# A fused attention and two-MLP kernel: the conversion of fp64 weight words moved off GpSimd, the second MLP's weights converted during the first and staged in device memory

## The chip, the core and the metric

The kernel runs on one core of one Trainium2 chip. The metric is the device time of the whole program in microseconds (us); a run takes some 1844 us.

## What is computed

Attention in chunks of 64 positions over q, k, v (batch 8, 8 heads, 576 positions, head size 64), then two MLPs on the 4608 resulting rows of 512 features. All weights arrive as fp64 words.

```python
attn = softmax(scale * q_c @ k_c^T)            # chunks of 64
x    = (attn @ v_c)                            # -> [4608, 512]
# first MLP, d_ff 1536
xn   = x / sqrt(mean(x*x) + 1e-6) * rms_g
g, v = xn @ w_gate, xn @ w_val
x    = (g * sigmoid(g) * v) @ w_out
# second MLP, d_ff 2048
h    = x @ w_in
P    = a0 + a1*h + a2*h^2 + a3*h^3
Q    = 1 + |b0|*|h| + |b1|*h^2
out  = (P / (Q + 1e-6)) @ w_out2
```

## The kernel before

The 4608 rows are worked in 9 blocks (`j`) of 512 rows. The first MLP runs over all blocks, then the second over all blocks; between them the rows wait in device memory (`x2d`). TensorE multiplies fp32 numbers as pairs: each operand is split into a rounded part (hi, type fp32r) and the remainder (lo), and each product is three matmuls of 128x512 (`PASSES`), so a product over 512 features is a group of 12 matmuls.

**First MLP.** In block `j`, for `f` in 0 to 11: `p1_gate` makes `g` (12 matmuls), ScalarE takes its tanh into `u` and VectorE multiplies (line 315); `p1_val` makes `vl` (12), VectorE multiplies (321), ScalarE casts hi of `r` (323) and VectorE subtracts for lo (324); `p1_gemm2` adds the product of an earlier `f` into the output accumulators `a` (12). `g` and `vl` share two PSUM buffers, so the next `g` needs the one that line 315 has read. Attention for the next block's four tiles of 128 rows is threaded between these groups by a plan of slots (three slots per `f`): matmuls `xs`, transposes `tp`, and work on VectorE, ScalarE and GpSimd. The first four tiles are done before the first block (`begin`, tiles named `start`).

**Second MLP.** Steps `s` over (`j`, `f`), `f` in 0 to 15: `h` (12 matmuls), a chain on ScalarE and VectorE, lo of `gg` on GpSimd (459), and three steps later `o` (12 matmuls).

**Weights.** `unit(u, w, keys)` brings three 128x512 weight tiles (1.5 MB of fp64 words) and converts them in place. Seen as 32-bit words, the high word is scaled by ScalarE as if it were fp32 (line 111) and the low word rounded to three bits (112). VectorE shifts the high word by three (114) and puts its sign back (115), GpSimd adds the two as integers (119), ScalarE casts hi (123), and lo is the difference (125), on VectorE for even units and on GpSimd for odd ones. 12 units serve the first MLP, 11 the second. The raw words and the converted pairs share 13 buffers of one size (`s3`), and the 12 units of the first MLP stay in them until its last block. So the units of the second MLP are converted in block 8, as the buffers of the first come free, and the tables `work` say at which slot each step of a unit is recorded.

In the first MLP a scheduler orders the instructions of each engine within these slots; in the second the order of ScalarE and VectorE is the written one. All DMAs are issued by SP, in one queue that waits in order.

Of the kernel before, what the change touches and what calls it, by code (L numbers as in the profile page):

```python
# [28 lines left out]
def fused_kernel(  # L29
# [66 lines left out]

    wt = {}

    def unit(u, w, keys):
# [6 lines left out]
        yield
        low, high = raw[:, :, :, 0], raw[:, :, :, 1]  # L110
# [462 lines left out]
```

## Time and profile before

| what | value |
|---|---|
| time, median of 3 runs | 1844.55 us (1843.34 to 1845.27) |
| the profiled execution: time, span | 1844.64 us, 1842.7 us |
| matmuls (PE) busy | 1779.6 us, 97% of the span |
| VectorE (DVE), ScalarE (ACT), GpSimd (POOL) busy | 1164.3, 901.5, 381.7 us |
| mean granted TensorE clock | 0.983 of full speed |

Time and span differ by 1.9 us, which lie around the profiled instructions. Busy time counts instructions that overlap at their ends as one; a matmul is in flight longer than the next one waits, so a busy PE is not a PE that could do no more. Where PE is gapless, the distance from one group of 12 matmuls to the next is the measure: 2.72 us.

### The profile page before, as it was taken

What the parts mean: (1) busy time and instruction counts of PE and PEld (TensorE: products, weight loads), DVE (VectorE), ACT (ScalarE), POOL (GpSimd) and SP (SyncE); (2) the same over time, 40 slices, a digit from 0 to 9 for tenths busy, and PEclk for the clock granted to TensorE, in tenths of its full rate; (3) what the DMA queues carried; (4) which work ended last, traced back from release to release, by engine and by line L of the source; (5) the groups of instructions that cost most, each with busy time, mean ns of one, the idle gap of its engine ahead of it and who ended that gap; (6) DMA issues with size and microseconds to landing.
All of it is one profiled execution on the core that took longest, in us unless ns stands there. A gap on an engine that the chain in (4) does not pass through costs nothing.

```text
span 1842.7 us, 24647 instructions
## 1 busy us (share of the span) xinstructions
PE 1779.6 (97%) x9948; PEld 1461.7 (79%) x9948; DVE 1164.3 (63%) x1602; ACT 901.5 (49%) x1408; POOL 381.7 (21%) x295
## 2 busy tenths in 40 slices
PE   4779999999999999999998899999999999999999
PEld 3668888888888888888887678888888888888887
DVE  6994444343344434434346698888787888888886
ACT  5653222222222222222235677767777776767675
POOL 3660000000000000000024442323232332233222
PEclk8889999999999999999999999999999999999999
DMA  7512111110011111101034400100101010101000
GB/s 297 200 52 69 58 34 42 35 58 24 30 58 35 42 34 58 30 23 58 1 115 140 149 20 5 42 29 18 35 12 35 12 40 7 40 7 46 1 23 23
DMA packets 41105, 93.86 MB, mean 51 GB/s; under 512 B 4640, under 2 KB 4640, under 8 KB 40992
## 3 DMA queue, kind: packets, MB, share of 16 engines
q1 hardware_dynamic: 40992, 92.30, 15.0%
q8 instruction: 78, 1.28, 0.3%
q14 instruction: 35, 0.29, 0.1%
HBM read 73.41 MB, written 18.87 MB: 50 GB/s over the span
## 4 chain that ended last, share of the span: by engine, by line
PE 87%; DVE 3%; issue 3%; POOL 2%; ACT 2%; POOLq 0%; DVEq 0%; ACTq 0%
PE o L469 21%; PE h L300 21%; PE g L300 14%; PE vl L300 14%; PE a L339 14%; PE xs L183 2%; POOL raw_i L119 1%; PE tp L228 1%; PE tp L225 1%; DVE raw_g L115 1%; POOL raw_q L119 0%; ACT w_i L123 0%; DVE r L324 0%; DVE t_g L114 0%; DVE raw_q L115 0%
## 5 line engine op out<-in xcount | busy, mean ns | idle before, releaser
L300 PE MATMUL g<-xT,w_g 128*128 128x512 f32 (+1 forms) x1308 | 320.1, 394 | 13.4 <-DVE u L315 11.3
L300 PE MATMUL vl<-xT,w_g 128*128 128x512 f32 x1296 | 322.1, 397 | 0.6 <-DVE u L321 0.6
L339 PE MATMUL a<-r,w_g 128*128 128x512 f32 x1296 | 316.5, 393 | 3.9 <-DVE r L324 2.7
L300 PEld LDWEIGHTS g<-xT,w_g 128*128 128x128 f32 x1308 | 248.2, 192 | 67.4 <-DVE u L315 13.6
L459 POOL TENSOR_TENSOR gg<-T,gg 128x512 fp32r<-128x512 f32 x144 | 187.5, 1302 | 509.7 <-ACT gg L458 417.4
L339 PEld LDWEIGHTS a<-r,w_g 128*128 128x128 f32 x1296 | 245.9, 190 | 56.4 <-DVE r L324 3.4
L300 PE MATMUL h<-x,w_i 128*128 128x512 f32 x1188 | 287.3, 391 | 2.9 <-DVE u L315 2.9
L315 DVE SCALAR_TENSOR_TENSOR u<-u,g 128x512 f32<-128x512 f32 x108 | 74.2, 687 | 341.5 <-ACT u L314 337.4
L300 PEld LDWEIGHTS vl<-xT,w_g 128*128 128x128 f32 x1296 | 241.1, 190 | 51.9 <-DVE u L321 1.8
L469 PE MATMUL o<-w_q,gg 128*128 128x512 f32 x1080 | 261.5, 391 | 2.3 <-ACT gg L458 1.4
L300 PEld LDWEIGHTS h<-x,w_i 128*128 128x128 f32 x1188 | 224.1, 189 | 50.0 <-DVE u L315 3.3
L469 PEld LDWEIGHTS o<-w_q,gg 128*128 128x128 f32 x1080 | 203.7, 189 | 45.5 <-ACT gg L458 1.9
L314 ACT ACTIVATE u<-g 128x512 f32<-128x512 f32 x108 | 64.6, 598 | 351.2 <-PE g L300 350.8
L438 ACT ACTIVATE V<-h 128x512 f32<-128x512 f32 x144 | 85.9, 596 | 181.7 <-PE h L300 181.5
L214 POOL TENSOR_SCALAR ssq<-ssq 128x1 f32<-128x1 f32 x36 | 8.8, 245 | 743.7 <-ACT xf L213 733.6
L469 PE MATMUL o<-w_i,gg 128*128 128x512 f32 x648 | 157.1, 391 | 0.0
L441 DVE SCALAR_TENSOR_TENSOR V<-V,small,R 128x512 f32<-128x512 f32 x144 | 108.3, 752 | 73.4 <-ACT R L439 73.4
L323 ACT CAST r<-u 128x512 fp32r<-128x512 f32 x108 | 67.1, 621 | 172.7 <-DVE u L321 172.6
L469 PEld LDWEIGHTS o<-w_i,gg 128*128 128x128 f32 x648 | 120.9, 188 | 27.7 <-DVE ob L480 2.3
L300 PE MATMUL h<-x,w_q 128*128 128x512 f32 x540 | 129.7, 389 | 0.0
L452 DVE SCALAR_TENSOR_TENSOR V<-V,R 128x512 f32<-128x512 f32 x144 | 125.6, 872 | 4.9
L451 DVE SCALAR_TENSOR_TENSOR V<-V,R 128x512 f32<-128x512 f32 x144 | 99.9, 693 | 44.9 <-ACT R L450 44.9
(118 smaller groups left out, 2032.3 us busy)
## 6 DMA issues: line engine op xcount, KB each, us to landing
raw_g<-in_w_dram SPq DMA_DIRECT2D x12, 1536.0 KB, 12.1
x2d<-x SPq DMA_DIRECT2D x36, 256.0 KB, 2.6
x2r<-x2d SPq DMA_DIRECT2D x36, 256.0 KB, 3.2
out_dram<-ob SPq DMA_DIRECT2D x36, 256.0 KB, 2.1
q<-in_qkv_dram SPq DMA_DIRECT2D x32, 256.0 KB, 2.7
k<-in_qkv_dram SPq DMA_DIRECT2D x32, 256.0 KB, 2.7
v<-in_qkv_dram SPq DMA_DIRECT2D x32, 256.0 KB, 2.9
raw_i<-in_w_dram SPq DMA_DIRECT2D x5, 1536.0 KB, 6.3
```

The costliest lines, as they stand in the source:

```text
L183: nc.tensor.matmul(out=ps[cc, hp, n, p, :], lhsT=lhsT, rhs=rhs, start=True, stop=True)
L300: nc.tensor.matmul(out=acc[:, ts], lhsT=w[:, wh, wk], rhs=x[:, kk, xh, ts], start=kk == 0 and n == 0, stop=kk == KD - 1 and n == 2,)
L314: nc.scalar.activation(out=u, in_=g, func=AF.Tanh, scale=0.5)
L315: nc.vector.scalar_tensor_tensor(out=u, in0=u, scalar=1.0, in1=g, op0=ALU.add, op1=ALU.mult)
L323: nc.scalar.copy(r[:, 0, :], u)
L339: nc.tensor.matmul(out=acc1[j][m], lhsT=wt["o", f][:, wh, ms], rhs=r[:, xh, :], start=f == 0 and n == 0, stop=f == NF1 - 1 and n == 2,)
L438: nc.scalar.activation(out=V, in_=h, func=AF.Square)
L441: nc.vector.scalar_tensor_tensor(out=V, in0=V, scalar=absb1, in1=R, op0=ALU.mult, op1=ALU.add)
L451: nc.vector.scalar_tensor_tensor(out=V, in0=V, scalar=1.0 + 1e-6, in1=R, op0=ALU.add, op1=ALU.mult)
L452: nc.vector.scalar_tensor_tensor(out=V, in0=V, scalar=-2.0, in1=R, op0=ALU.add, op1=ALU.mult)
L459: nc.gpsimd.tensor_tensor(out=r[:, 1, :], in0=T, in1=r[:, 0, :].bitcast(F32), op=ALU.subtract)
L469: nc.tensor.matmul(out=acc2[j][m], lhsT=r[:, rh, ms], rhs=wt["q", f][:, wh, :], start=f == 0 and n == 0, stop=f == NF2 - 1 and n == 2,)
```

## The change

The conversion becomes one helper, `words_to_pair`, on ScalarE and VectorE alone. ScalarE's first operation is Prelu with a slope for negative numbers: it scales a negative high word by another power of two than a positive one, so that the shift by three leaves the sign bit where it belongs. With that the operation that put the sign back is gone. The integer add of high and low is an instruction of VectorE (named ISA in the order, its operands as 1536 times 2 halves of a word), and lo is VectorE's for every unit. Unit 0 is brought and converted in three parts.

The second MLP's weights no longer wait for block 8. Each of the 32 tiles is a generator `stage(t)`: 512 KB come into the 13th buffer, the only one left beside the 12 units, are converted there, and the pair (512 KB) is written to device memory (`w2d`). In block 8 `unit2` loads three finished pairs by one DMA as each buffer comes free.

```diff
-    def unit(u, w, keys):
+    def words_to_pair(high, low, t, hi, lo):
+        nc.scalar.activation(
+            out=high.bitcast(F32), in_=high.bitcast(F32), func=AF.Prelu, scale=2.0 ** -112, alpha=2.0 ** 32
+        )
+        nc.scalar.mul(t.bitcast(I32), low, 2.0 ** -29)
+        yield
+        nc.vector.tensor_scalar(out=high, in0=high, scalar1=3, scalar2=None, op0=ALU.logical_shift_left)
+        nc.vector.tensor_tensor(out=high, in0=high, in1=t, op=ALU.add)
+        yield
+        x = high.bitcast(F32)
+        nc.scalar.copy(hi, x)
+        nc.vector.tensor_tensor(out=lo, in0=x, in1=hi.bitcast(F32), op=ALU.subtract)
+        yield
+
+    def unit(u, keys):
...
-        nc.scalar.mul(high.bitcast(F32), high.bitcast(F32), 2.0 ** -112)
-        nc.scalar.mul(low.bitcast(I32), low, 2.0 ** -29)
-        t = sb.tile([P, U, W], U32, tag="t", bufs=1, name=f"t_{name}")[:, :n]
-        nc.vector.tensor_scalar(out=t, in0=high, scalar1=3, scalar2=None, op0=ALU.logical_shift_left)
-        nc.vector.scalar_tensor_tensor(
-            out=high, in0=high, scalar=0x80000000, in1=t, op0=ALU.bitwise_and, op1=ALU.bitwise_or
-        )
-        yield
-        nc.gpsimd.tensor_tensor(out=high.bitcast(I32), in0=high.bitcast(I32), in1=low.bitcast(I32), op=ALU.add)
...
-        nc.scalar.copy(whole[:, :n, 0, :], x)
-        eng = (nc.vector, nc.gpsimd)[u % 2]
-        eng.tensor_tensor(out=whole[:, :n, 1, :], in0=x, in1=whole[:, :n, 0, :].bitcast(F32), op=ALU.subtract)
...
+        parts = [slice(t, t + 1) for t in range(n)] if u == 0 else [slice(0, n)]
...
+    w2d = [dram.tile([P, U, 2, W], F32, tag=f"w2d_{u}", name=f"w2d_{u}") for u in range(-(-2 * NF2 // U))]
+
+    def stage(t):
+        buf = s3(f"stage{t}")
+        raw = buf[:, 0].rearrange("p two f -> p (two f)").bitcast(U32)
+        pair = buf[:, 1]
+        nc.sync.dma_start(out=raw, in_=w2[t])
+        yield
+        raw = raw.rearrange("p (f two) -> p f two", two=2)
+        for _ in words_to_pair(raw[:, :, 1], raw[:, :, 0], buf[:, 2, 0].bitcast(U32), pair[:, 0, :], pair[:, 1, :]):
+            yield
+        nc.sync.dma_start(out=w2d[t // U][:, t % U], in_=pair.bitcast(F32))
+        yield
+
+    def unit2(u, keys):
+        whole = s3(f"w2_{u}")
+        n = len(keys)
+        nc.sync.dma_start(out=whole[:, :n].bitcast(F32), in_=w2d[u][:, :n])
...
+        span = (NB - 2) * 3 * NF1
+        for t in range(2 * NF2):
+            at = 3 * NF1 + t * span // (2 * NF2)
+            at_slots(stage(t), (at, at + 2, at + 3, at + 4, at + 5))
         for u, x in enumerate(second):
-            for at in (3 * u + 6 if u else 0, 3 * u + 8, 3 * u + 9, 3 * u + 10):
-                work.setdefault((NB - 1, at), []).append(x)
+            at_slots(x, ((NB - 1) * 3 * NF1 + 3 * u,))
```

The lines of the changed kernel have other numbers: the shift is 110, the add 111, lo 115; Prelu 105, the low word 108, the cast 114; tanh 347, the VectorE steps on `u` and `r` 348, 354 and 357, the cast of `r` 356.

**VectorE in the first block, `f` = 0 and 1** (before, then with the change; `raw_g_3` is unit 3's words, `w_g_2` unit 2's pair, `u0_1` block 0, `f` = 1). Before:

```order
L125 TENSOR_TENSOR w_g_2_499<-raw_g_2_106,w_g_2_499 128x3x512
L321 TENSOR_TENSOR u0_0_438<-u0_0_438,vl0_0_441 128x512
L114 TENSOR_SCALAR t_g_3_472<-raw_g_3_411 128x1536
L115 SCALAR_TENSOR_TENSOR raw_g_3_411<-raw_g_3_411,t_g_3_472 128x1536
L324 TENSOR_TENSOR r0_0_455<-u0_0_438,r0_0_455 128x512
L315 SCALAR_TENSOR_TENSOR u0_1_490<-u0_1_490,g0_1_477 128x512
L114 TENSOR_SCALAR t_g_4_536<-raw_g_4_475 128x1536
L321 TENSOR_TENSOR u0_1_490<-u0_1_490,vl0_1_502 128x512
L115 SCALAR_TENSOR_TENSOR raw_g_4_475<-raw_g_4_475,t_g_4_536 128x1536
L324 TENSOR_TENSOR r0_1_516<-u0_1_490,r0_1_516 128x512
```

With the change:

```order
L354 TENSOR_TENSOR u0_0_461<-u0_0_461,vl0_0_464 128x512
L270 RECIPROCAL den4_490<-den4_490 128x8
L111 ISA raw_g_3_433<-raw_g_3_433,t_g_3_494 128x1536x2
L357 TENSOR_TENSOR r0_0_478<-u0_0_461,r0_0_478 128x512
L115 TENSOR_TENSOR w_g_2_122<-raw_g_2_121,w_g_2_122 128x3x512
L348 SCALAR_TENSOR_TENSOR u0_1_513<-u0_1_513,g0_1_500 128x512
L110 TENSOR_SCALAR raw_g_4_497<-raw_g_4_497 128x1536
L354 TENSOR_TENSOR u0_1_513<-u0_1_513,vl0_1_524 128x512
L115 TENSOR_TENSOR w_g_3_434<-raw_g_3_433,w_g_3_434 128x3x512
L357 TENSOR_TENSOR r0_1_538<-u0_1_513,r0_1_538 128x512
L111 ISA raw_g_4_497<-raw_g_4_497,t_g_4_557 128x1536x2
```

The steps on `u` and `r` stand among the conversions as before, and the units are as far ahead. Per unit there were two VectorE instructions and, for every other unit, a third; now there are always three, and none on GpSimd between the second and the cast.

**ScalarE in block 1, `f` = 5 to 7** (`u1_5` is block 1, `f` = 5; `xf` and `p` are attention). Before:

```order
L314 ACTIVATE u1_5_1740<-g1_5_1727 128x512
L323 CAST r1_5_1763<-u1_5_1740 128x512
L314 ACTIVATE u1_6_1791<-g1_6_1778 128x512
L213 ACTIVATE xf10_1829,ssq10_1830<-xa10_1827 128x512
L200 ACTIVATE p11_1834<-p11_1834 128x512
L323 CAST r1_6_1853<-u1_6_1791 128x512
L314 ACTIVATE u1_7_1881<-g1_7_1868 128x512
```

With the change:

```order
L347 ACTIVATE u1_5_1773<-g1_5_1760 128x512
L105 ACTIVATE stage8_2904<-stage8_2904 128x512
L108 ACTIVATE stage8_2904<-stage8_2904 128x512
L356 CAST r1_5_1796<-u1_5_1773 128x512
L114 CAST stage8_2904<-stage8_2904 128x512
L347 ACTIVATE u1_6_1828<-g1_6_1815 128x512
L246 ACTIVATE xf10_1866,ssq10_1867<-xa10_1864 128x512
L105 ACTIVATE stage9_3083<-stage9_3083 128x512
L233 ACTIVATE p11_1871<-p11_1871 128x512
L108 ACTIVATE stage9_3083<-stage9_3083 128x512
L356 CAST r1_6_1892<-u1_6_1828 128x512
L114 CAST stage9_3083<-stage9_3083 128x512
```

Each `f` has the three ScalarE operations of one staged tile between its tanh and the next. The scheduler has put the 32 tiles earlier than their slots say: tile 0 behind the tanh of block 0, `f` = 7, tile 31 behind that of block 3, `f` = 8, so 31 tiles further on in 37 steps of `f`.

**SP in block 2** (`stage16` is tile 16's buffer, `w2d_5` the pairs of tiles 15 to 17). Before:

```order
L353 DMA x2d_1_69<-x2_1_0_2279 128x512
L353 DMA x2d_1_69<-x2_1_1_2282 128x512
L353 DMA x2d_1_69<-x2_1_2_2285 128x512
L353 DMA x2d_1_69<-x2_1_3_2288 128x512
L164 DMA q14_2373<-in_qkv_dram 128x512
L165 DMA k14_2374<-in_qkv_dram 128x512
L166 DMA v14_2375<-in_qkv_dram 128x512
```

With the change:

```order
L150 DMA stage16_4440<-in_w2_dram 128x1024
L155 DMA w2d_5_82<-stage16_4440 128x1024
L150 DMA stage17_4626<-in_w2_dram 128x1024
L155 DMA w2d_5_82<-stage17_4626 128x1024
L150 DMA stage18_4818<-in_w2_dram 128x1024
L197 DMA q15_2653<-in_qkv_dram 128x512
L198 DMA k15_2654<-in_qkv_dram 128x512
L199 DMA v15_2655<-in_qkv_dram 128x512
L155 DMA w2d_6_83<-stage18_4818 128x1024
```

Loading and writing alternate, one tile at a time, in the one queue, with the loads for attention between them.

**ScalarE in the last block, `f` = 7 to 9.** Before:

```order
L111 ACTIVATE raw_q_7_7553<-raw_q_7_7553 128x1536
L314 ACTIVATE u8_7_7568<-g8_7_7555 128x512
L112 ACTIVATE raw_q_7_7553<-raw_q_7_7553 128x1536
L323 CAST r8_7_7588<-u8_7_7568 128x512
L123 CAST w_q_7_7627<-raw_q_7_7553 128x3x512
L314 ACTIVATE u8_8_7624<-g8_8_7611 128x512
L111 ACTIVATE raw_i_9_7609<-raw_i_9_7609 128x1536
L112 ACTIVATE raw_i_9_7609<-raw_i_9_7609 128x1536
L323 CAST r8_8_7644<-u8_8_7624 128x512
L123 CAST w_i_9_7683<-raw_i_9_7609 128x3x512
L111 ACTIVATE raw_q_10_7665<-raw_q_10_7665 128x1536
```

With the change:

```order
L347 ACTIVATE u8_7_7831<-g8_7_7818 128x512
L356 CAST r8_7_7848<-u8_7_7831 128x512
L347 ACTIVATE u8_8_7878<-g8_8_7865 128x512
L356 CAST r8_8_7895<-u8_8_7878 128x512
L347 ACTIVATE u8_9_7925<-g8_9_7912 128x512
L356 CAST r8_9_7942<-u8_9_7925 128x512
```

The conversions between the steps on `u` and `r` are gone. Loads of ScalarE's tables are as many as before (two).

## Rows read from the trace of the kernel before

**Rows 1.** The page: busy tenths of PE in 40 slices of 46 us
```profile
PE   4779999999999999999998899999999999999999
```

**Rows 2.** Stretches: us, busy (instructions) by engine, granted clock, DMA share, GB/s
```profile
42.00:145.00 103.00, 83.57 (x531) 66.74 (x532) 93.38 (x76) 60.32 (x61) 60.11 (x23) 0.84 0.37 131
145.00:955.00 810.00, 810.00 (x5351) 668.85 (x5350) 332.51 (x553) 199.35 (x350) 25.77 (x60) 1.00 0.13 41
955.00:1110.00 155.00, 140.15 (x573) 112.13 (x572) 116.62 (x119) 100.13 (x125) 71.14 (x32) 0.94 0.30 104
```

**Rows 3.** PE in order of time, start of the kernel: start us, us, instruction
```profile
39.86 0.58 PE L300 MATMUL g<-xT,w_g 128*128 128x256 f32 x1
...
142.29 2.89 PE L339 MATMUL a<-r,w_g 128*128 128x512 f32 x12
```

**Rows 4.** A stretch without conversions, in order of time, as in rows 3
```profile
439.61 2.88 PE L300 MATMUL g<-xT,w_g 128*128 128x512 f32 x12
...
443.16 0.69 DVE L315 SCALAR_TENSOR_TENSOR u<-u,g 128x512 f32<-128x512 f32 x1 [4.00 <-ACT u L314]
...
447.77 2.88 PE L300 MATMUL g<-xT,w_g 128*128 128x512 f32 x12
```

**Rows 5.** The chain that ended last: start us, us, piece
```profile
451.74 2.95 PE vl L300 x12
...
478.44 2.95 PE vl L300 x12
```

**Rows 6.** DVE from 42 to 145 us: busy us, mean ns, idle before
```profile
L115 DVE SCALAR_TENSOR_TENSOR raw_g<-raw_g,t_g 128x1536 uint32<-128x1536 uint32 x9 | 20.2, 2246 | 0.1
L114 DVE TENSOR_SCALAR t_g<-raw_g 128x1536 uint32<-128x1536 uint32 x9 | 16.5, 1838 | 0.3 <-ACT raw_g L111 0.3
L324 DVE TENSOR_TENSOR r<-u,r 128x512 fp32r<-128x512 f32 x7 | 15.4, 2199 | 1.5 <-ACT r L323 1.5
L125 DVE TENSOR_TENSOR w_g<-raw_g,w_g 128x1536 fp32r<-128x1536 f32 x5 | 11.0, 2196 | 0.5 <-ACT w_g L123 0.5
...
L250 DVE TENSOR_TENSOR xT<-start,xT 128x512 fp32r<-128x512 f32 x1 | 3.7, 3665 | 1.6 <-ACT xT L248 1.6
L250 DVE TENSOR_TENSOR xT<-xf,xT 128x512 fp32r<-128x512 f32 x2 | 3.5, 1748 | 0.6 <-ACT xT L248 0.6
```

**Rows 7.** DVE from 145 to 955 us, as in rows 6
```profile
L324 DVE TENSOR_TENSOR r<-u,r 128x512 fp32r<-128x512 f32 x92 | 64.2, 697 | 44.4 <-ACT r L323 44.4
```

**Rows 8.** Instructions on raw_g: duration ns min/median/max, first and last start
```profile
L114 DVE TENSOR_SCALAR t_g<-raw_g x12: 948/960/3497, 13.8 to 121.5; 128x1536 uint32<-128x1536 uint32 x12
L115 DVE SCALAR_TENSOR_TENSOR raw_g<-raw_g,t_g x12: 1745/1759/3701, 14.8 to 123.7; 128x1536 uint32<-128x1536 uint32 x12
L119 POOL TENSOR_TENSOR raw_g<-raw_g x12: 2742/2746/3546, 16.7 to 126.8; 128x1536 int32<-128x1536 int32 x12
```

**Rows 9.** ACT from 42 to 145 us, as in rows 6
```profile
L123 ACT CAST w_g<-raw_g 128x1536 fp32r<-128x1536 f32 x10 | 16.4, 1635 | 26.3 <-POOL raw_g L119 21.5 <-DVE w_g L125 4.8
L111 ACT ACTIVATE raw_g<-raw_g 128x1536 f32<-128x1536 f32 x9 | 14.7, 1638 | 0.0
```

**Rows 10.** PE in order of time, end of the first MLP
```profile
957.30 2.88 PE L339 MATMUL a<-r,w_g 128*128 128x512 f32 x12
...
980.26 5.49 PE L300 MATMUL g<-xT,w_g 128*128 128x512 f32 x12 [3.41 <-DVE u L315]
...
1107.76 2.88 PE L469 MATMUL o<-w_q,gg 128*128 128x512 f32 x12
```

**Rows 11.** Who waited for whom, 955 to 1110 us: us, times, longest
```profile
PE g L300 <- DVE u L315: 9.1, 3, 4.0
```

**Rows 12.** DMA issues: engine, count, KB each, median us to landing
```profile
x2d<-x SPq DMA_DIRECT2D x36, 256.0 KB, 2.6
...
raw_i<-in_w_dram SPq DMA_DIRECT2D x5, 1536.0 KB, 6.3
...
raw_i<-in_w_dram SPq DMA_DIRECT2D x1, 1024.0 KB, 4.8
```

More of the change, by code (lines that the diff above doesn't have):

```diff
@@ new lines, in unit @@
+    def unit(u, keys):
+        name, n = "_".join(map(str, keys[0])), len(keys)
+        raw = s3(f"raw_{name}", (P, U, W, 2), U32)
+        whole = s3(f"w_{name}")
+        parts = [slice(t, t + 1) for t in range(n)] if u == 0 else [slice(0, n)]
+        for p in parts:
+            nc.sync.dma_start(
+                out=raw[:, p].rearrange("p t f two -> p t (f two)"),
+                in_=w1[u * U:u * U + n][p].rearrange("t p f -> p t f"),
+            )
+        yield
+        low = sb.tile([P, U, W], U32, tag="t", bufs=1, name=f"t_{name}")
+        stages = [
+            words_to_pair(raw[:, p, :, 1], raw[:, p, :, 0], low[:, p], whole[:, p, 0, :], whole[:, p, 1, :])
+            for p in parts
+        ]
+        for t, key in enumerate(keys):
+            wt[key] = whole[:, t]
+        for _ in range(3):
+            for x in stages:
+                next(x)
+            yield
@@ L120, in unit @@
         yield
-        whole = s3(f"w_{name}")
-        x = high.bitcast(F32)
-        nc.scalar.copy(whole[:, :n, 0, :], x)
-        eng = (nc.vector, nc.gpsimd)[u % 2]
-        eng.tensor_tensor(out=whole[:, :n, 1, :], in0=x, in1=whole[:, :n, 0, :].bitcast(F32), op=ALU.subtract)
+    def unit2(u, keys):
+        whole = s3(f"w2_{u}")
+        n = len(keys)
+        nc.sync.dma_start(out=whole[:, :n].bitcast(F32), in_=w2d[u][:, :n])
         for t, key in enumerate(keys):
@@ L128, in unit @@
         yield
-    def units(w, keys):
-        return [unit(u, w, keys[u * U:(u + 1) * U]) for u in range(-(-len(keys) // U))]
     X = {}
@@ L369, in fused_kernel, with split, at_slots @@
     with ExitStack():
-        first = units(w1, [(n, f) for f in range(NF1) for n in "gvo"])
-        second = units(w2, [(n, f) for f in range(NF2) for n in "iq"])
+        def split(keys):
+            return [keys[n:n + U] for n in range(0, len(keys), U)]
+        first = [unit(u, keys) for u, keys in enumerate(split([(n, f) for f in range(NF1) for n in "gvo"]))]
+        second = [unit2(u, keys) for u, keys in enumerate(split([(n, f) for f in range(NF2) for n in "iq"]))]
         work = {}
+        def at_slots(x, slots):
+            for at in slots:
+                work.setdefault(divmod(at, 3 * NF1), []).append(x)
         for u, x in enumerate(first):
-            for at in (3 * u - 9, 3 * u - 6, 3 * u - 4, 3 * u - 2)[u == 2:] if u > 1 else ():
-                work.setdefault((0, at), []).append(x)
+            at_slots(x, (3 * u - 9, 3 * u - 6, 3 * u - 4, 3 * u - 2)[u == 2:] if u > 1 else ())
+        span = (NB - 2) * 3 * NF1
+        for t in range(2 * NF2):
+            at = 3 * NF1 + t * span // (2 * NF2)
+            at_slots(stage(t), (at, at + 2, at + 3, at + 4, at + 5))
         for u, x in enumerate(second):
-            for at in (3 * u + 6 if u else 0, 3 * u + 8, 3 * u + 9, 3 * u + 10):
-                work.setdefault((NB - 1, at), []).append(x)
+            at_slots(x, ((NB - 1) * 3 * NF1 + 3 * u,))
         def weights(j, at):
@@ L494, in fused_kernel @@
                     p2_first(s)
-                    weights(NB - 1, 3 * NF1 + 2 * s)
-                    weights(NB - 1, 3 * NF1 + 2 * s + 1)
+                    weights(NB, s)
                 if s == 0:
```

5 lines of the change are left out of this document (removed).

## Prediction

> **What bounds the kernel now.** I read the page first. Its row of TensorE's busy tenths is full but for two places, the first three slices (up to some 138 us) and the 22nd and 23rd (some 967 to 1060 us) [rows 1]. By stretches: from 145 to 955 us TensorE is busy for 810.0 of 810 us at full clock, so there nothing but fewer matmuls would help; from 42 to 145 us it has 83.6 of 103 at a mean clock of 0.84, and from 955 to 1110 us 140.2 of 155 at 0.94 [rows 2]. In both of these VectorE is the busy one: 93.4 of 103 and 116.6 of 155, with GpSimd at 60.1 and 71.1. Both are the places of the conversions.
>
> How much is lost there is counted in groups of 12 matmuls. In a stretch without conversions three groups take 447.77 - 439.61 = 8.16 us, 2.72 each [rows 4]. Three steps of `f` with one attention tile take 478.44 - 451.74 = 26.70 us [rows 5], so a tile costs 26.70 - 9 x 2.72 = 2.22 us, and a step of `f` 8.90 on average.
>
> First place: from the first `g` at 39.86 to the end of the `a` that starts at 142.29 are 105.3 us [rows 3]. They hold 23 groups (8 `g`, 8 `vl`, 7 `a`) and about three attention tiles, 62.6 + 6.7 = 69.2 us. Lost: 36.1 us. Second place: from the `a` at 957.30 to the `o` at 1107.76 are 150.5 us for 46 groups, 125.1 us [rows 10]. Lost: 25.3 us. There the wait is `g` for VectorE's step on `u`, 9.1 us in three waits [rows 11]; the rest is clock: after one idle time of 3.41 us a group took 5.49 us where others take 2.88 [rows 10]. So a stall costs its length and about 2.6 us more.
>
> Why VectorE is full in the first place is seen in its groups. The shift takes 960 ns and the sign step 1759 ns in the median [rows 8], but 1838 and 2246 in the mean here, and the subtraction for `r`, 697 ns in the long stretch [rows 7], takes 2199 [rows 6]. The extra time: conversions 47.7 us busy (20.2 + 16.5 + 11.0) against 9 x 1.76 + 9 x 0.96 + 5 x 1.75 = 33.2, so 14.5; `r` 15.4 - 7 x 0.70 = 10.5; the three subtractions for `xT` 7.2 - 3 x 0.70 = 5.1. Together 30 us of VectorE's 93.4, on instructions that read two tensors or write the shift. Such long ones are not found where GpSimd is nearly idle (25.8 of 810 us), so I take them for the two engines standing in each other's way. ScalarE's cast waits for GpSimd's add as well, 21.5 us [rows 9].
>
> **The change, part by part.** *GpSimd's add and half the lo subtractions go.* 12 + 11 adds of 2.75 us leave GpSimd [rows 8], and with them the extra 30 us of VectorE. Its other work in this stretch is then 93.4 - 47.7 - 10.5 - 5.1 = 30.1 us.
>
> *VectorE gets an add, every lo, and loses the sign step.* By the order, up to the `r` of `f` = 6, which the last `a` of this stretch needs, VectorE has 10 shifts, 10 adds and 8 subtractions of units 2 to 11. Shift 0.96, subtraction 1.75. The add is not in the trace. Below, it is the sign step, two tensors of the same shapes and the same spacing, 1.76. Above: the order gives its operands as 1536 x 2 halves, and if each half takes an element's time, then by (1759 - 697) / 1024 = 1.04 ns an element (1536 against 512 columns) [rows 7, 8] it is 1.76 + 1536 x 1.04 = 3.36. I take the lower, being the nearest row. VectorE then needs 9.6 + 17.6 + 14.0 + 30.1 = 71.3 us, or 87.3 with the slow add, beside TensorE's 69.2. So the two are level, and neither hides the other's waits fully. I add 5 us for one stall of some 2.4 and the slow group behind it: 76 us, between 69 and 92. Saved: 105.3 - 76 = **29** (13 to 36).
>
> [...]
>
> *Prelu for the multiplication.* Taken as equal, 1.64 us [rows 9]; ScalarE is busy for 60 of 103 us [rows 2] and its table loads stay two, so 0.3 us more in each of ten would be hidden by the 26.3 us that it now idles before its casts.
>
> *Unit 0 in three parts, before the first `g`.* ScalarE's exponentials for the first tiles now stand behind parts of unit 0, and GpSimd's add no longer holds `xT` back. I take 0, between -3 and +2, which is one or two instructions of 1.6 us either way.
>
> *Block 8 without conversions.* Between the tanh steps of block 8 only the casts of `r` stay. The pairs come by DMA alone: 11 loads of up to 1.5 MB, 6.3 us each [rows 12], one per 8.2 us of matmuls, each behind the buffer that a finished `f` frees, three units ahead of need or more. What stays is the filling of the second MLP's pipeline; I leave 1.5 of the 25.3 us. Saved: **24** (18 to 25).
>
> *32 staged tiles in blocks 0 to 3.* ScalarE and VectorE each get about 1.7 us per tile; they are busy for 199 and 333 of 810 us [rows 2]. The danger is the single buffer: tile after tile goes through load, conversion, write, one at a time, and ScalarE and VectorE take their instructions in order, with the next tanh behind a tile that has not come. One round: load 3.3 (1536 KB take 6.3, 1024 KB 4.8, so 512 KB 1.5 less [rows 12]), Prelu and low word 2 x 0.55 (a third of rows 9), add 0.70, cast 0.6, subtraction 0.70, write 2.6 + 0.75 (256 KB more at the same rate) [rows 12]; 9.8 us, and some 0.4 for six handovers: 10.2. The order has 31 rounds in 37 steps of `f`: 37 x 8.90 / 31 = 10.6 us each. It fits by 0.4. And VectorE frees a `g` buffer at 443.85, 3.9 us before the next `g` needs it [rows 4], so small delays are hidden. Cost taken: 0; if the round were longer, 31 times the excess less 3.9 us.
>
> **Sum.** The profiled execution took 1844.64 us, 0.1 above the median of the runs. 1844.6 - 29 - 24 = **1792 us** (1791.6).
>
> **Rivals.** *Slow add, 3.36 us.* For it: it is a new instruction on halves of words. Against: rows 8. The start takes 87.3 + 5 = 92 us and saves 13; a staging round is 0.55 longer, 10.75, 31 x 0.15 = 4.7 against 3.9 of cover. 1844.6 - 13 - 24 + 1 = 1809 us. [...]
>
> *Staging sets the pace.* One mechanism, in blocks 0 to 3: a round longer than 10.6 us delays ScalarE's tanh, and TensorE waits for `g`'s buffer. For it: the margin is 0.4 us, SP's one queue also holds the loads for attention, which wait for buffers, and a tile's write stands behind them. Against: those buffers come free with `tp`, ahead of the tile's last step. At 11.5 us: 31 x 0.9 - 3.9 = 24 us, 1816 us. From 10.6 + (53 + 3.9) / 31 = 12.4 us on, the kernel is **slower** than before, by 31 us for each further microsecond.
>
> *The start hardly gains.* If VectorE's long instructions are not GpSimd's doing, it keeps them and gets the lo subtractions too; what goes then is only the casts' wait. I give it 10 us for 29: 1811 us.
>
> *Start at TensorE's pace.* No stall at all, and 3 us won ahead of `g`: 1844.6 - 36 - 25 - 3 = 1781 us.
>
> **How the numbers follow.** Forecast 0.58 (1785 to 1800), TensorE's pace 0.08, slow add 0.10, small gain at the start 0.07, staging between 10.6 and 12.4 us 0.12, beyond that 0.05. From 1780 to 1816 lie the first four and a third of the fifth, 0.87; some of the forecast's own ends lie outside. A change within 0.2% (3.7 us) is about what a measurement of this kernel cannot tell from none. Only the last case is slower by more: 0.05; same 0.01, faster 0.94.
>
> **What the changed profile would show.** Right: a subtraction for `r` of 0.7 us from 42 to 145 us, the 23rd group ended by some 116 us, no wait of `g` for `u` in block 8, `h` without the 25 us, and TensorE full in blocks 1 to 3. Wrong, and where: the add at more than 2 us; TensorE waiting for VectorE's `u` in blocks 1 to 3 with ScalarE's Prelu waiting for the DMA of a staged tile; `h` or `o` waiting for a DMA of `w2`; VectorE's steps long with GpSimd idle.

## The result, and the profile after

The changed kernel takes **1793.76 us** in the median of 4 runs (1790.37 to 1795.54), against 1844.19 us before; the ratio is 0.9724, with a 95% interval of 0.9707 to 0.9741. The prediction was 1792, between 1780 and 1816. The sum came out right; one of its three terms did not. The rows below are of the profiled execution, the longest of the four (1795.54 us).

The page of the changed kernel, busy tenths of TensorE and its granted clock in 40 slices of 45 us. The two dips of [rows 1] are gone but for the first slice:

```profile
PE   4999999999999999999999999999999999999998
...
PEclk8999999999999999999999999999999999999999
```

The same three stretches as [rows 2], in the same columns:

```profile
42.00:145.00 103.00, 102.49 (x706) 84.37 (x705) 87.68 (x114) 70.83 (x82) 5.59 (x8) 0.99 0.41 151
145.00:955.00 810.00, 805.48 (x5253) 662.32 (x5252) 364.37 (x623) 240.65 (x427) 26.18 (x60) 1.00 0.25 87
955.00:1110.00 155.00, 154.46 (x681) 127.36 (x680) 102.72 (x142) 88.20 (x142) 30.20 (x24) 1.00 0.21 77
```

The first and third are full now, with GpSimd at 5.6 us where it had 60.1. The middle one, which had no gap at all, now has 4.5 us in which TensorE is idle.

Where the time came from is read from the starts of the same groups in both kernels. TensorE of the changed kernel in order of time (start, us, instruction):

```profile
37.39 0.58 PE L333 MATMUL g<-xT,w_g 128*128 128x256 f32 x1
...
48.31 3.00 PE L333 MATMUL g<-xT,w_g 128*128 128x512 f32 x12
...
109.46 2.88 PE L372 MATMUL a<-r,w_g 128*128 128x512 f32 x12
...
422.77 2.88 PE L333 MATMUL g<-xT,w_g 128*128 128x512 f32 x12
...
932.31 2.88 PE L372 MATMUL a<-r,w_g 128*128 128x512 f32 x12
...
1058.29 2.88 PE L512 MATMUL o<-w,gg 128*128 128x512 f32 x12
```

They answer to the `g` at 39.86 and the `a` at 142.29 [rows 3], the `g` at 447.77 [rows 4] (block 3, `f` = 6), and the `a` at 957.30 and the `o` at 1107.76 [rows 10]. (The row at 48.31 is the second `g`, at 53.19 before.) The lead of the changed kernel at each is the difference:

| place | lead, us | what was forecast |
|---|---|---|
| first `g` | 2.5 | 0 |
| seventh `a`, end of the start | 32.8 | 29 |
| block 3, `f` = 6 | 25.0 | 29 |
| block 8, `a` at 932.31 | 25.0 | 29 |
| `o` at step 8 of the second MLP | 49.5 | 53 |

So the start gives 32.8 us, blocks 0 to 3 take 7.8 of it back, and block 8 gives 24.5. From there to the end the lead stays.

VectorE of the changed kernel from 42 to 145 us, to be held against [rows 6] (busy us, mean ns):

```profile
L115 DVE TENSOR_TENSOR w_g<-raw_g,w_g 128x1536 fp32r<-128x1536 f32 x10 | 17.5, 1752 | 1.0 <-ACT w_g L114 0.8
L111 DVE CUSTOM_DVE_ANT_0 raw_g<-raw_g,t_g 128x3072 uint16<-128x3072 uint16 x10 | 17.5, 1749 | 0.9 <-ACT t_g L108 0.8
L110 DVE TENSOR_SCALAR raw_g<-raw_g 128x1536 uint32<-128x1536 uint32 x9 | 8.5, 950 | 0.0
...
L357 DVE TENSOR_TENSOR r<-u,r 128x512 fp32r<-128x512 f32 x11 | 7.5, 685 | 1.6 <-ACT r L356 1.6
```

The new add takes 1.749 us. The shift is back from 1.84 to 0.95, lo from 2.20 to 1.75, the subtraction for `r` from 2.20 to 0.69.

### The profile page after: what moved, and what is told of

It reads as the page before. It is cut to its first block, busy times and chain, and to the rows that moved or that the text cites. A ratio compares the mean times of both kernels' runs of the same rounds, so it can differ in the third digit from the quotient of the medians.

```text
span 1793.4 us, 24893 instructions
## 1 busy us (share of the span) xinstructions
PE 1760.2 (98%) x9948; PEld 1448.9 (81%) x9948; DVE 1136.0 (63%) x1682; ACT 909.9 (51%) x1477; POOL 271.2 (15%) x261
## 3 DMA queue, kind: packets, MB, share of 16 engines
q1 hardware_dynamic: 47552, 125.85, 19.9%
## 4 chain that ended last, share of the span: by engine, by line
PE 78%; DMA 10%; DVE 4%; ACT 4%; issue 3%; POOL 1%; SPq 0%; ACTq 0%; POOLq 0%
PE o L512 22%; PE h L333 21%; PE vl L333 11%; PE g L333 11%; PE a L372 10%; DMA stage<-in_w_dram 5%; DMA w2d<-stage 4%; PE xs L216 1%; DVE stage L115 1%; ACT stage L105 1%; DVE stage L111 1%; ACT stage L108 1%; DMA start<-in_qkv_dram 1%; PE tp L261 1%; ACT stage L114 1%
## 5 line engine op out<-in xcount | busy, mean ns | idle before, releaser
L512 PE MATMUL o<-w,gg 128*128 128x512 f32 x1728 | 416.2, 390 | 0.5 <-POOL gg L502 0.5
L333 PE MATMUL h<-x,w 128*128 128x512 f32 x1728 | 414.9, 389 | 0.0
L512 PEld LDWEIGHTS o<-w,gg 128*128 128x128 f32 x1728 | 323.5, 188 | 70.3 <-DVE ob L523 2.3
L333 PEld LDWEIGHTS h<-x,w 128*128 128x128 f32 x1728 | 324.3, 188 | 67.4
L333 PE MATMUL g<-xT,w_g 128*128 128x512 f32 (+1 forms) x1308 | 314.6, 389 | 4.1 <-DVE u L348 2.6
L372 PE MATMUL a<-r,w_g 128*128 128x512 f32 x1296 | 311.6, 389 | 0.0
L483 ACT ACTIVATE T<-h,small 128x512 f32<-128x512 f32 x144 | 112.4, 780 | 0.0
L496 DVE SCALAR_TENSOR_TENSOR T<-T,small,V 128x512 f32<-128x512 f32 x144 | 108.3, 752 | 5.1
L486 DVE SCALAR_TENSOR_TENSOR T<-T,small,h 128x512 f32<-128x512 f32 x144 | 107.7, 748 | 5.1
```

The lines of the kernel that those rows point to most:

```text
L333: nc.tensor.matmul(out=acc[:, ts], lhsT=w[:, wh, wk], rhs=x[:, kk, xh, ts], start=kk == 0 and n == 0, stop=kk == KD - 1 and n == 2,)
L372: nc.tensor.matmul(out=acc1[j][m], lhsT=wt["o", f][:, wh, ms], rhs=r[:, xh, :], start=f == 0 and n == 0, stop=f == NF1 - 1 and n == 2,)
L483: nc.scalar.activation(out=T, in_=h, func=AF.Identity, scale=a3, bias=a2)
L486: nc.vector.scalar_tensor_tensor(out=T, in0=T, scalar=a1, in1=h, op0=ALU.add, op1=ALU.mult)
L496: nc.vector.scalar_tensor_tensor(out=T, in0=T, scalar=a0, in1=V, op0=ALU.add, op1=ALU.mult)
L512: nc.tensor.matmul(out=acc2[j][m], lhsT=r[:, rh, ms], rhs=wt["q", f][:, wh, :], start=f == 0 and n == 0, stop=f == NF2 - 1 and n == 2,)
```

## Experiments

Two theories for the start and block 8 stood against each other: that GpSimd's long instructions stretched VectorE's (A), and that the loss was GpSimd's place in the chain of a conversion (B), or the attention steps queued behind its long instructions (C). For blocks 0 to 3: that ScalarE waits in order for a tile's load (A), or that the tiles' work as such costs (B). A lead below is always read as in the table above.

**Without staging** (e_nostage). The second MLP's weights are converted in block 8 again, by the new helper.

```diff
-        for t in range(2 * NF2):
-            at = 3 * NF1 + t * span // (2 * NF2)
-            at_slots(stage(t), (at, at + 2, at + 3, at + 4, at + 5))
...
-            at_slots(x, ((NB - 1) * 3 * NF1 + 3 * u,))
+            at_slots(x, [(NB - 1) * 3 * NF1 + at for at in (3 * u + 6 if u else 0, 3 * u + 8, 3 * u + 9, 3 * u + 10)])
```

> The second MLP's weights are converted in the last block again, at the slots of the kernel before, but by the new helper without GpSimd. Both theories: the start keeps its 32.8 us, blocks 0 to 3 keep TensorE full, so the 7.8 us that they lose with staging are back. Theory A (the last block lost its 25 us because GpSimd's add and subtractions stretched VectorE's instructions and stood in the chain): VectorE needs 27 us without conversions in that block and 11 x 4.46 = 49 more, 76 of 98 us, a smaller share than in the start, which runs without a stall; the block loses 6 us or less, and the time is 1786 to 1793 us: staging is worth nothing. Rival B (the last block lost it to the conversions as such: late loads and three engines in one chain): it loses some 20 to 25 us again, 1806 to 1811 us.

Measured: 1796.44 us, ratio 0.974 (0.9725 to 0.9754), 2.7 us above the changed kernel; the intervals of the two ratios overlap, but its runs (1796.27 to 1797.69) all lie above those of the changed kernel. The time is past theory A's 1793. Stretches of this kernel, block 8 and what follows:

```profile
895.90:993.80 97.90, 97.90 (x433) 81.09 (x432) 63.75 (x63) 58.39 (x57) 7.37 (x4) 1.00 0.50 171
993.80:1059.50 65.70, 60.58 (x253) 49.22 (x252) 56.85 (x72) 49.90 (x76) 18.48 (x14) 0.95 0.13 41
```

Block 8 converts nine of the eleven units and TensorE has no gap in it: 97.9 of 97.9 us. What remains is one wait at the second MLP's first `o`, and the slow group behind it:

```profile
1004.70 2.88 PE L333 MATMUL h<-x,w_i 128*128 128x512 f32 x12
1012.44 0.79 PE L509 MATMUL o<-w_i,gg 128*128 128x512 f32 x1 [4.86 <-ACT gg L498]
1013.03 5.32 PE L333 MATMUL h<-x,w_i 128*128 128x512 f32 x12
```

The idle 4.86 us and 5.32 - 2.72 us for the group make 7.5. The lead is 31.5 us ahead of block 8 and 48.2 at `o`: 16.7 of the 24.5 us come from the helper alone. The helper changes more than GpSimd's share, and no run takes it apart in block 8: that GpSimd is the cause there is carried over from the start, where s_dummy below shows it. In the window 895 to 994 us the subtraction for `r` takes 0.84 us in the mean, where it took 1.52 before from 955 to 1060 us. Theory A holds in kind; its "6 us or less" was 7.8 by the leads.

**Staging alone** (e_stageonly): the kernel before, with `stage` and `unit2` of the changed kernel and its helper for the staged tiles only.

```diff
+            at, x = 3 * NF1 + t * span // (2 * NF2), stage(t)
+            for k in (at, at + 2, at + 3, at + 4, at + 5):
+                work.setdefault(divmod(k, 3 * NF1), []).append(x)
...
-            for at in (3 * u + 6 if u else 0, 3 * u + 8, 3 * u + 9, 3 * u + 10):
-                work.setdefault((NB - 1, at), []).append(x)
+            work.setdefault(divmod((NB - 1) * 3 * NF1 + 3 * u, 3 * NF1), []).append(x)
```

> The kernel before with only the second part of the change: 32 staged tiles (by the new helper) and loads of finished pairs in the last block; the first MLP's weights are converted as before. If the two parts add up: 1844.2 + 7.8 - 24.5 = 1827.5 us, with the start's subtraction for r still near 2.2 us. If staging costs more where GpSimd is still at the first MLP's weights, or the loss in blocks 0 to 3 comes from the new start, it lies more than 3 us beside that.

Measured: 1825.55 us, ratio 0.9896. The forecast was 1827.5, so the parts add up within 2 us: by its leads 1.6 at the seventh `a`, -5.4 in block 3, 18.9 at `o`.

**Tiles spread over blocks 1 to 7** (e_spread). Prelu and the low word's step of a staged tile are held behind what is recorded ahead of them on ScalarE (`keep` is `tc.keep_in_program_order` for staged tiles).

```diff
-        nc.scalar.activation(
+        keep(nc.scalar.activation(
...
-        )
-        nc.scalar.mul(t.bitcast(I32), low, 2.0 ** -29)
+        ))
+        keep(nc.scalar.mul(t.bitcast(I32), low, 2.0 ** -29))
```

> The changed kernel with ScalarE's first two operations of a staged tile held behind what is recorded ahead of them, so that the 32 tiles lie over blocks 1 to 7, one per 2.6 steps of f, and each load is issued a step or more before ScalarE comes to it. Theory A (TensorE loses 7.8 us in blocks 0 to 3 because ScalarE waits in order for the load of a tile, 99 us in 26 waits, and tanh and the exponentials stand behind): the waits vanish, 1794 - 7.8 = 1786 us. Rival B (each tile costs 0.25 us by its work on ScalarE and VectorE and its DMA traffic): 32 x 0.25 stays, 1794 us.

Measured: **1787.24 us** (1787.00 to 1787.69), ratio 0.9689. The lead is 32.9 us at the seventh `a`, 32.6 in block 3 and 32.6 ahead of block 8; TensorE in blocks 1 to 7:

```profile
145.00:905.00 760.00, 760.00 (x5065) 627.47 (x5064) 361.43 (x616) 237.87 (x421) 20.68 (x56) 1.00 0.24 84
```

The same 32 tiles with the same instructions and bytes cost nothing when ScalarE comes to a tile that has landed: no wait of ScalarE for a tile's load is left. Rival B is out. The edit also puts the tiles 24 us apart instead of 10.66, so the runs don't part the waiting from the crowding.

How the changed kernel lost the 7.8 us is seen in its rounds. One of the long ones, all engines, instructions of the staged tiles and two of attention:

```profile
264.40 0.33 SPq L150 DMA_DIRECT2D stage<-in_w_dram  x1
268.13 0.68 ACT L105 ACTIVATE stage<-stage 128x512 f32<-128x512 f32 x1 [5.70 <-DMA stage<-in_w_dram]
268.71 0.62 ACT L246 ACTIVATE xf<-xa 128x512 f32<-128x512 f32 x1
...
269.95 0.63 ACT L233 ACTIVATE p<-p 128x512 f32<-128x512 f32 x1
273.61 0.42 SPq L155 DMA_DIRECT2D w2d<-stage  x1
276.64 0.33 SPq L150 DMA_DIRECT2D stage<-in_w_dram  x1
```

ScalarE stands idle for 5.70 us for the load, with attention's two activations and the next tanh queued behind. This round takes 12.24 us from load to load, the one before it (254.76 to 264.40) 9.64. All 32 loads lie between 114.1 and 444.5 us, 10.66 us apart on average and 9.6 to 13.0 in single rounds (the view of the staged tile's instructions: ns min/median/max, first and last start):

```profile
L150 SPq DMA_DIRECT2D stage<-in_w_dram x32: 327/328/377, 114.1 to 444.5; - x32
```

Waits of the changed kernel from 148 to 423 us (who waited for whom, us in total, times, longest):

```profile
ACT stage L105 <- DMA stage<-in_w_dram: 99.2, 26, 6.3
...
PE g L333 <- DVE u L348: 2.6, 2, 1.3
...
PE tp L261 <- ACT p L233: 1.1, 3, 0.4
```

The round above reached TensorE hardly at all; its lead falls there by 0.25 us. It falls at seven waits, 4.5 us of idle time in all, by 0.65 to 1.5 us each with the slower groups around them. One of the two of `g`, all engines:

```profile
364.14 0.66 ACT L105 ACTIVATE stage<-stage 128x512 f32<-128x512 f32 x1 [2.67 <-DMA stage<-in_w_dram]
...
366.70 0.58 ACT L347 ACTIVATE u<-g 128x512 f32<-128x512 f32 x1
...
367.44 0.68 DVE L348 SCALAR_TENSOR_TENSOR u<-u,g 128x512 f32<-128x512 f32 x1
...
368.17 3.02 PE L333 MATMUL g<-xT,w_g 128*128 128x512 f32 x12 [1.32 <-DVE u L348]
```

ScalarE comes to the tile 2.67 us before its words have landed, the tanh of `u` stands behind the tile, and TensorE's `g` behind VectorE's step on `u`. The other five are attention's: `tp` four times and `xs` once, for the load of `k`.

**Two buffers for raw words** (e_tworaw).

```diff
-        buf = s3(f"stage{t}")
-        raw = buf[:, 0].rearrange("p two f -> p (two f)").bitcast(U32)
+        if not ring:
+            ring.extend((s3("stage"), sb.tile([P, U, W], U32, tag="t", bufs=1, name="t_stage")))
+        buf, low = ring
+        raw = buf[:, 2 * (t % 2)].rearrange("p two f -> p (two f)").bitcast(U32)
...
-        for _ in words_to_pair(raw[:, :, 1], raw[:, :, 0], buf[:, 2, 0].bitcast(U32), pair[:, 0, :], pair[:, 1, :]):
+        for _ in words_to_pair(raw[:, :, 1], raw[:, :, 0], low[:, t % 2], pair[:, 0, :], pair[:, 1, :]):
```

> The changed kernel with two buffers for the raw words of staged tiles (two thirds of the same 13th buffer; the scaled low word goes into the tile that the first MLP's units used), so that a load is issued while the tile before is converted; the scheduler then places 1.45 tiles per step of f instead of 0.84. Theory A: a load needs 3.4 us and a tile's turn is now 6.1 us, ScalarE waits less for loads, and most of the 7.8 us come back: 1786 to 1790 us. Rival B, work as such: 1794 us. If the write to device memory, 2.6 us, which the next tile's cast must now wait for, takes the load's place: 1794 us or more, with ScalarE's cast waiting for that DMA.

Measured: 1792.76 us (1791.13 to 1794.76), not to be told from the changed kernel. The lead falls from 31.9 to 27.3 us between the seventh `a` and block 3, by 4.7 instead of 7.8. ScalarE's waits between 110 and 420 us are 26.1 us for loads, and 19.9 for the write of the tile before. An earlier load alone doesn't do it where the scheduler then packs the tiles closer.

The next ones are edits of e_spread, whose runs lie within 0.7 us.

**Idle work on GpSimd** (s_dummy).

```diff
-        for _ in range(3):
+        for k in range(3):
...
+            if k == 1 and u > 2:
+                words = raw[:, :, :, 0].bitcast(I32)
+                nc.gpsimd.tensor_tensor(out=words, in0=words, in1=words, op=ALU.add)
```

> The kernel of e_spread (1787.2 us) with one more GpSimd instruction for each of units 3 to 11: it doubles the unit's low words in place, 128x1536 int32 of the shapes of the old add, after they have been used; nothing reads the result and only the buffer's next use waits for it. Theory A (GpSimd's conversions stretched VectorE's instructions, 30 us in 105): 9 x 2.75 = 25 us of GpSimd give VectorE 25 x 30 / 51 = 14 us more (51 us of GpSimd before: 30.5 + 24.7 less what it still has to do), it needs 83 us for 75, the subtraction for r takes well over 0.7 us beside them, and the start is longer by some 8 us: 1795 us. Rival B (the gain came from GpSimd's place in the chain of a unit's conversion): VectorE's instructions keep their lengths, 1787 us.

Measured: 1803.66 us, 16.4 more than e_spread for nine instructions whose result nobody reads. VectorE from 42 to 145 us:

```profile
L111 DVE CUSTOM_DVE_ANT_0 raw_g<-raw_g,t_g 128x3072 uint16<-128x3072 uint16 x10 | 24.0, 2396 | 0.8 <-ACT t_g L108 0.7
L115 DVE TENSOR_TENSOR w_g<-raw_g,w_g 128x1536 fp32r<-128x1536 f32 x10 | 19.0, 1897 | 0.5 <-ACT w_g L114 0.4
...
L351 DVE SCALAR_TENSOR_TENSOR u<-u,g 128x512 f32<-128x512 f32 x10 | 6.8, 680 | 4.4 <-ACT u L350 4.4
...
L279 DVE TENSOR_SCALAR xa<-xa,ssq 128x512 f32<-128x512 f32 x4 | 4.4, 1102 | 1.7 <-POOL ssq L251 1.6
```

The add and lo are longer (2.40 and 1.90 us, each 1.75 in the changed kernel), the step on `u`, which reads PSUM, is not (0.680 for 0.683). Theory A's direction holds, but the price is twice the forecast 8 us, and TensorE waited longest for `tp` behind `xa` and `ssq` (8.7 us in three waits), which GpSimd's queue could explain. So that was taken apart:

**The same with `ssq` off GpSimd** (q_dummy), and its control without the idle work (q_ssq). `ssq` is the sum of squares of an attention tile's rows.

```diff
-        nc.gpsimd.tensor_scalar(out=ssq, in0=ssq, scalar1=1.0 / DM, scalar2=1e-6, op0=ALU.mult, op1=ALU.add)
-        nc.gpsimd.tensor_tensor(out=ssq, in0=ssq, in1=mhalf, op=ALU.pow)
+        eng = nc.gpsimd if t.start else nc.vector
+        eng.tensor_scalar(out=ssq, in0=ssq, scalar1=1.0 / DM, scalar2=1e-6, op0=ALU.mult, op1=ALU.add)
+        eng.tensor_tensor(out=ssq, in0=ssq, in1=mhalf, op=ALU.pow if t.start else ALU.max)
```

> The kernel of s_dummy, which took 1803.7 us (16.4 more than e_spread), with attention's two small steps on ssq on VectorE instead of GpSimd for all tiles but the first four (the power is left out and a maximum stands in its place, so these rows are scaled by another number). In s_dummy TensorE waited 8.7 us in three waits for tp behind VectorE's scaling of xa, which waits for ssq, and ssq stands in GpSimd's queue behind the idle additions. Theory A (VectorE's stretched instructions are the loss): the stretch of VectorE stays, some 14 us, and most of the 16.4 us too: 1797 to 1804 us. Theory C (the queue: small steps of attention behind long instructions of GpSimd): 1788 to 1794 us, with VectorE's instructions as long as in s_dummy.

> The control for q_dummy: e_spread with the same change of ssq and without the idle additions (the power is left out here too). All theories: 1787 us, within 1.5; VectorE has two short instructions more per attention tile, 0.2 to 0.3 us each.

Measured: 1802.82 and 1787.71 us: 15.1 us for the idle work with no queue in between. Theory C is out; 1.3 us of the 16.4 may be the queue's. No other instruction waited for one of the nine. From 37 to 140 us VectorE's instructions grew against the control by 15.0 us (the subtraction for `r` by 7.5, the add 4.1, the shift 1.9, lo 1.5), which is near theory A's 14 us; the forecast took nearly half of it as hidden, and none was. VectorE of q_dummy in order of time:

```profile
64.76 1.76 DVE L111 CUSTOM_DVE_ANT_0 raw_g<-raw_g,t_g 128x3072 uint16<-128x3072 uint16 x1 [0.33 <-ACT t_g L108]
66.43 0.69 DVE L241 TENSOR_TENSOR xa<-xs,den 128x512 f32<-128x512 f32 x1
...
67.63 0.68 DVE L358 TENSOR_TENSOR u<-u,vl 128x512 f32<-128x512 f32 x1
...
69.27 1.75 DVE L115 TENSOR_TENSOR w_g<-raw_g,w_g 128x1536 fp32r<-128x1536 f32 x1
70.95 3.22 DVE L361 TENSOR_TENSOR r<-u,r 128x512 fp32r<-128x512 f32 x1
```

And its GpSimd:

```profile
64.80 4.32 POOL L143 TENSOR_TENSOR raw_g<-raw_g 128x1536 int32<-128x1536 int32 x1 [7.19 <-ACT t_g L108]
69.97 3.65 POOL L143 TENSOR_TENSOR raw_g<-raw_g 128x1536 int32<-128x1536 int32 x1 [0.84 <-ACT t_g L108]
```

In these rows they take turns, by whole instructions. The GpSimd add of 64.80 lasts till 69.12, which is 2.60 after the end of L111 at 66.52; the second lasts till 73.62, again 2.60 after the end of L115 at 71.02; and the subtraction for `r` lasts till 74.17, 0.55 after that. Between them `xa` and `u`, which read one tensor from PSUM, take 0.69 and 0.68 us while GpSimd works, for 0.68 in the mean in the changed kernel from 42 to 145 us. Each of the two engines waits for the other here: 3.22 us for a subtraction of 0.69, and 4.32 us for an add of 2.75 [rows 8].

**The integer add on GpSimd again** (s_addpool), for the first MLP's units.

```diff
-        nc.vector.tensor_tensor(out=high, in0=high, in1=t, op=ALU.add)
...
+            eng.tensor_tensor(out=high.bitcast(I32), in0=high.bitcast(I32), in1=t.bitcast(I32), op=ALU.add)
```

> The kernel of e_spread with the integer add of the first MLP's units on GpSimd again (Prelu and no sign operation, every lo on VectorE). VectorE loses 10 x 1.75 = 17.5 of its 69 us in the start. Theory A: 10 adds of 2.75 to 3.05 us stretch it by some 16 us, so that it needs about what it needed, 68 us for 75, and the start is only a little longer through the handovers to and from GpSimd: 1787 to 1792 us. Rival B (the chain through GpSimd is what cost): ScalarE's casts wait for the add as before, and the start loses most of the 30 us: over 1800 us.

Measured: 1805.79 us, 18.6 more, though VectorE lost ten adds. This theory A did not foresee. Waits of this kernel from 37 to 140 us:

```profile
ACT t_g L108 <- POOL raw_g L112: 10.2, 5, 4.3
...
PE g L336 <- DVE u L351: 8.9, 5, 3.2
ACT w_g L117 <- POOL raw_g L112: 8.8, 3, 4.1
```

VectorE is busy for 76.9 of 93.3 us there, lo at 2.85 us in the mean; the adds, 3.75 us each with their turns, now stand in the chain of a unit too, and ScalarE waits for them with TensorE's tanh behind. So both theories have a share where GpSimd's instruction is part of the chain; how much each has in these 18.6 us, the runs don't tell.

**Every other lo on GpSimd** (s_lopool).

```diff
-        nc.vector.tensor_tensor(out=lo, in0=x, in1=hi.bitcast(F32), op=ALU.subtract)
+        eng.tensor_tensor(out=lo, in0=x, in1=hi.bitcast(F32), op=ALU.subtract)
...
-            words_to_pair(raw[:, p, :, 1], raw[:, p, :, 0], low[:, p], whole[:, p, 0, :], whole[:, p, 1, :])
+            words_to_pair(raw[:, p, :, 1], raw[:, p, :, 0], low[:, p], whole[:, p, 0, :], whole[:, p, 1, :], eng=(nc.vector, nc.gpsimd)[u % 2])
```

> The kernel of e_spread with lo of every other unit on GpSimd again, as before the change. VectorE loses 5 x 1.75 = 8.75 us of work in the start; GpSimd gets 5 or 6 subtractions, which took 4.1 us each before the change. Theory A: they stretch VectorE's instructions by 25 x 30 / 51 = 14 us, net 5 us more, 74 us for 75: 1787 to 1792 us. Theory C (queue of ssq): one or two waits of 3 us for tp, and 1790 to 1796 us. If taking work off VectorE is what counts: 1787 us or less.

Measured: 1794.71 us, 7.5 more, with five subtractions off VectorE: past A's bound, and in C's range, with 4.0 us of waits for `tp`. The subtraction for `r` is 1.25 us, the shift 1.32, GpSimd's lo 4.2. Work taken off VectorE cost time here, where GpSimd got it.

**The sign step back on VectorE** (s_sign).

```diff
...
+        if sign:
+            nc.vector.scalar_tensor_tensor(
+                out=t, in0=high, scalar=0x80000000, in1=t, op0=ALU.bitwise_and, op1=ALU.bitwise_or
+            )
+        nc.vector.tensor_tensor(out=high, in0=low if sign else high, in1=t, op=ALU.add)
```

> The kernel of e_spread with the sign operation back on VectorE for the first MLP's units (Prelu with a slope of one, the shift into the tile of the low word, sign put back there, then the add): 1.76 us more per unit. VectorE then needs 69 + 10 x 1.76 = 86.5 us in a start of 75. If VectorE is the next bound there: 12 to 17 us longer, 1799 to 1804 us. If the start only needed GpSimd's relief and VectorE's work has room: 1787 to 1790 us.

Measured: 1794.63 us, 7.4 more, less than the 12 to 17. From its first `g` to the end of the seventh `a`:

```profile
41.72:115.98 74.26, 72.36 (x535) 60.06 (x534) 72.35 (x80) 54.27 (x57) 10.76 (x8) 0.95 0.45 160
```

These are 74.3 us, as without the step (74.6), with VectorE at 72.4: what doesn't fit is put off to the units that are needed later. The loss lies on either side, 4.1 us ahead of the first `g` (41.72 for 37.65) and the rest around one wait behind this stretch (`tp` for `xa`, 2.1 us at 119.88).

Put back one at a time, the add on GpSimd costs 18.6 us, lo 7.5 and the sign step 7.4, 33.5 together, near the 32.9 us that the start gained. Such single prices need not add up, but the sign step's share is not small beside GpSimd's two.

**Unit 0 whole** (s_unit0).

```diff
-        parts = [slice(t, t + 1) for t in range(n)] if u == 0 else [slice(0, n)]
+        parts = [slice(0, n)]
```

> The kernel of e_spread with unit 0 brought and converted whole. The changed kernel's first g starts 2.5 us earlier and its first step takes 2.4 us less than before. If the split made this: 1787.2 + 2.5 to 4.9 = 1790 to 1792 us. If it came from GpSimd, whose add no longer stands ahead of its work for xT: 1787 us.

Measured: 1788.01 us (1787.13 to 1789.54), 0.8 more, which is hardly told from none; the first `g` is at 38.43. So the split is not what made the first `g` earlier, 2.2 us in e_spread. GpSimd's add isn't either: with it back (s_addpool) the first `g` is at 37.50. The edit that moves it most is the sign step, 41.72 in s_sign.

**Unit 1 behind the first attention tiles** (b_late).

```diff
-START = "01a23bc" "0a123" "01a23" "01a23" "b0123" "b0123" "b"
+START = "01a23bc" "0a123" "01a23" "01a23" "b0123" "0123b" "b"
...
+                          late=tc.keep_in_program_order if u == 1 else lambda x: x)
```

> The kernel of e_spread with unit 1's shift held behind VectorE's steps for the first four attention tiles. In e_spread GpSimd's two small steps on ssq, 0.19 and 0.55 us when alone, take 1.65 and 2.04 us where VectorE adds or subtracts for unit 1 at the same time, and the first g waits for these tiles. Theory A (the two engines take turns by whole instructions): both are short again, the first g starts 1.5 to 3 us earlier than 37.65, and VectorE, with 69 of 75 us, and gapless even with the sign step's 14.5 us more, catches up: 1784.2 to 1785.7 us. Rival: the conversions put off are missed later, or another step of the tiles ends last: 1787 us or more.

Measured: **1783.75 us** (1783.03 to 1784.19), ratio 0.9666 (0.9653 to 0.9679), the fastest version here. GpSimd of e_spread, the steps on `ssq` of two tiles:

```profile
27.01 2.04 POOL L248 TENSOR_TENSOR ssq<-ssq,small 128x1 f32<-128x1 f32 x1
...
33.53 1.65 POOL L247 TENSOR_SCALAR ssq<-ssq 128x1 f32<-128x1 f32 x1 [1.29 <-ACT start L246]
```

The same two of b_late, and its first `g` (from TensorE's view):

```profile
27.34 0.56 POOL L249 TENSOR_TENSOR ssq<-ssq,small 128x1 f32<-128x1 f32 x1
...
31.17 0.19 POOL L248 TENSOR_SCALAR ssq<-ssq 128x1 f32<-128x1 f32 x1
```

```profile
33.83 0.58 PE L334 MATMUL g<-xT,w_g 128*128 128x256 f32 x1
```

VectorE of e_spread at the same times:

```profile
26.88 1.76 DVE L111 CUSTOM_DVE_ANT_0 raw_g<-raw_g,t_g 128x3072 uint16<-128x3072 uint16 x1
...
33.39 1.75 DVE L115 TENSOR_TENSOR w_g<-raw_g,w_g 128x1536 fp32r<-128x1536 f32 x1
```

A step on one element per partition waited 1.5 us for VectorE's long add and another as long for its subtraction. The turns go both ways. The first `g` is 3.8 us earlier, past theory A's 1.5 to 3: the edit also takes ScalarE's cast for unit 1 (1.58 us at 31.24 in e_spread) out from between the tiles' steps, and this run does not part the two.

## Why the prediction was right, and where not

**The bound, and GpSimd's part in it: right.** The step that takes 30 us of VectorE's 93.4 for the two engines standing in each other's way carried most of the forecast. s_dummy and q_dummy show it by itself: nine adds that nobody waits for cost 15 to 16 us. Not all of the start's 32.8 us is this: s_sign puts 7.4 of them down to the sign step. That r came back to 0.69 us, as was named, is its mark in the changed profile. The rival "the start hardly gains" is out.

**The add: right at the lower bound.** 1.749 us for 1.76 taken. The upper estimate, 3.36 us with an element's time for each half, does not hold for this instruction in this trace.

**The start: right size, 76 for 75 us, by a partly wrong reason.** The 5 us for a stall lie in the first step: the first `g` and `vl` take 48.31 - 37.39 = 10.9 us for 5.4 us of matmuls. Behind that are 64.0 us for 21 groups and three tiles, 57.1 + 6.7: no stall. "So the two are level, and neither hides the other's waits fully" was too cautious, since VectorE can put off units that TensorE needs later; s_sign has 72.4 us of VectorE's work in 74.3. The slow-add rival's 92 us are then likely too long as well: s_sign, with 17.6 us more for VectorE, lost 7.4. And 2.5 us were won ahead of the first `g`, where 0 was taken with a gain of 3 at most.

**The staged tiles: the step that failed.** "It fits by 0.4" and "Cost taken: 0" measured 7.8 us. The mean round was 10.66 us, where 10.2 was forecast and 10.6 was to be had, so nothing of the 0.4 was left. The other 0.4, for six handovers, was the author's estimate and no row shows it; in the round at 254.76 us the four handovers from the low word's step to the write took 0.03 us each. And the step compared means: rounds ran from 9.6 to 13.0, the longest with attention's activations in between, and a short one gives nothing back, because ScalarE waits for the next load anyway (26 waits, 99 us). The 3.9 us of cover were read for `g` alone; five of the seven waits are attention's `tp` and `xs`, whose cover was not read. This is the rival "Staging sets the pace" in mechanism and place, at a third of the price given there; e_spread shows that it is ScalarE's waiting at this spacing, not the work of the tiles.

**Block 8: right size, 24.5 for 24, credited to the wrong part.** It was put down to conversions leaving the block. e_nostage keeps them there and gains 16.7 us by the helper, most likely through GpSimd's absence. Staging adds 7.8 in block 8 and takes 7.8 in blocks 0 to 3, so as ordered it is worth nothing that these leads show, and 2.7 us by the times. The loss there before the change was misread too, "the rest is clock": TensorE was idle for 14.9 of the 155 us [rows 2], so 5.8 beside the 9.1 of `g` were other waits, of `h` for `u` (2.9) and of `o` for `gg` (2.3) above all.

The sum came so near by some luck: two errors of opposite sign met, 3.8 us more at the start and 7.8 less in blocks 0 to 3. Either alone would have stayed within the range.

## What to carry to other kernels

Before giving work to an idle GpSimd, look at how long VectorE's instructions of the same shape are beside it and without it; here the idle engine cost more than the busy one saved (s_addpool: 18.6 us more, with ten adds of 1.75 us off VectorE). Work that is prefetched in order through one buffer is judged by its longest round against the steps beside it, not by the mean, and an instruction that waits for a transfer should be queued when the transfer has landed, not when the buffer is free. And take the parts of a change apart even where the sum is right.
